# Inducing-point attention and a PReLU layer: token loads and second-attention scores moved to other groups of a hand-ordered schedule

## The chip, the cores and the metric

One core of one Trainium2 chip runs the whole kernel in one launch. The metric is the device time of that core in microseconds (us); the median of five runs of the kernel before is 597.24 us.

The core has TensorE (PE, with weight loads on a row of its own, PEld), VectorE (DVE), ScalarE (ACT), GpSimd (POOL) and SyncE (SP). DMAs are issued in program order from the queues of SP and POOL.

## The reference

Four batches of 12480 tokens with 128 channels attend to and from 32 inducing points; the result runs through a layer of 2048 hidden channels with a PReLU.

```python
B, N, m, C = (4, 12480, 32, 128)
def mab(q, kv):
    s = scale * (q @ kv.transpose(0, 2, 1))
    s = s - s.max(-1, keepdims=True)
    a = np.exp(s)
    a /= a.sum(-1, keepdims=True) + 1e-09
    return a @ kv
h = mab(I, x)              # first attention: 32 inducing points over all tokens of a batch
y = mab(x, h)              # second attention: every token over the 32 rows of h
hid = y @ w_in             # 128 -> 2048
g = np.maximum(hid, 0.0) + alpha * np.minimum(hid, 0.0)
out = g @ w_out            # 2048 -> 128
```

The first attention of a batch must be finished before the second one of that batch starts, so the kernel works on batch n's second attention and layer while it prepares h for batch n+1.

## The kernel before, in words

**Tiles.** A batch is cut into six supers of 2048 tokens (unit numbers 0 to 5) and a remainder of 192 tokens (unit 6). A super has four groups of 512 tokens, and the remainder is a group of its own: 25 groups in a batch, numbered 0 to 24. In the text, "1:17" is group 17 of the second batch (batches count from 0).

**Fills.** The main loop runs over (batch, group, j). One pass of it is a *slot*: j goes over 0 to 3 in a full group and over 0 and 1 in the last, so a batch has 98 slots. In a slot `fill` (L446) makes four matmuls `ring<-rep,hW` (the rows of the second attention's exponentials, `rep`, times h·w_in, `hW`), each into a bank of its own out of a ring of six; ACT (L470) or DVE (L472) empties each bank through a ReLU into `gt`. Then the slot's tasks run, and `mm2` (L476) multiplies the slot before by w_out (`W1`), accumulating 512 tokens of the output in `acc`. The linear part of the PReLU is one 128x128 matrix `Amat`, made at the start by `w_amat` (L684) from `AW` = alpha·w_out and `winT` = the transposed w_in; `linear` (L517) adds it once a group.

**Out.** After a group's last slot, `turn` (L559) lets DVE transpose `acc` into `yT`. When all four groups of a super are there, 16 shuffle DMAs `yq<-yT` (L572) and four `leave` steps (L579 multiplies by the reciprocal denominators, L589 stores) are put on a list, and each slot takes two of its entries. All 20 are POOL's, in order.

**Tasks.** `at(slot, fn, j, cost, narrow)` puts a step into slot (group, j), j being 1 unless it is given. Steps of the next batch's first attention, one of each for each unit u, in the order 0, 1, 6, 2, 3, 4, 5:
- `a_load` (L126): the load of x from HBM with a cast, issued by POOL, not before the ACT instruction that precedes it in the program (`after`);
- `a_xpose` (L155): a transposing DMA `xT<-xn` on SP (L158; L163 for unit 6);
- `a_scores` (L271): four matmuls `ring<-xT,IT`, an exponential on ACT (L277), and a transposing DMA `e1T<-e` on SP (L281);
- `a_accum` (L295): sixteen small matmuls `ring<-xn,e1T` and an addition on DVE (L308).

Steps of the current batch's second attention for each super s: `b_scores` (L363; matmuls `ring<-xT,hT`, an exponential, a store of it to DRAM on SP, L379), `b_rep` (L382; four DMAs back into `rep`, L387), `b_den` (L402; denominators). The order on each engine is pinned to program order (`pin`); semaphores for data and for the reuse of buffers are put in by the framework. A planner (`make_plan`) shares out the evictions between ACT and DVE from the steps' costs.

**Narrow slots.** Where a step with matmuls 32 columns wide runs, `mm2` is issued as 16 matmuls of 32 columns (forms 128*32) in place of four of 128 (128*128).

**Buffers** that matter here: `xn` six, `xT` two (one a batch), `e1T` two, `rep` three, `e2` two, `yT` three, `yq` two, `ob` four.

Of the kernel before, what the change touches and what calls it, by code (L numbers as in the profile page):

```python
# [15 lines left out]
P = 128  # L16
NB = 4
GRP = P * NB
NQ = 4
# [5 lines left out]
def kernel(  # L25
# [11 lines left out]
    bf16 = mybir.dt.bfloat16  # L37

    B, N, C = x.shape
# [9 lines left out]
    KC = DFF // P  # L49
# [20 lines left out]

    const = ctx.enter_context(tc.tile_pool(name="const", bufs=1))
    work = ctx.enter_context(tc.tile_pool(name="work", bufs=2))
    xn_pool = ctx.enter_context(tc.tile_pool(name="xnp", bufs=6))
    xt_pool = ctx.enter_context(tc.tile_pool(name="xtp", bufs=2))
    gt_pool = ctx.enter_context(tc.tile_pool(name="gtp", bufs=4))
    head_pool = ctx.enter_context(tc.tile_pool(name="headp", bufs=3))
# [78 lines left out]
    def a_xpose(st, u):  # L155
        xn = st.xn[u]
        if u < NS:
            pin(nc.sync.dma_start_transpose(  # L158
                out=st.xT[:, u, :, :].rearrange("c q (j p) -> c (q j) p", j=NB),
                in_=xn[:].rearrange("p q f -> p (q f)"),  # L160
            ))
        else:
            pin(nc.sync.dma_start_transpose(  # L163
                out=st.xTr[:], in_=xn[:].rearrange("p j c -> p (j c)")
            ))
# [216 lines left out]
    def b_rep(st, s, q0=0):  # L382
        nq, w = (NQ, GRP) if s < NS else (1, REM)
        rep = rep_pool.tile([P, nq, w], bf16, name="rep", tag="rep" if s < NS else "repr")
        dv = st.d.pop(s)[:].rearrange("(q i) t -> i q t", q=nq)
        for r in range(4):
            pin(nc.sync.dma_start(out=rep[32 * r : 32 * r + 32, q0:], in_=dv[:, q0:]))  # L387
        for q in range(q0, nq):
            st.rep[s * NQ + q] = rep[:, q, :]
# [12 lines left out]
    def b_den(st, s):  # L402
        e2 = st.e2.pop(s)
        ps = bank()
        if s < NS:
            for j in range(NB):
                mm(ps[:, j * NQ : (j + 1) * NQ], e2[:, j * P : (j + 1) * P], pick[:])
            rd = rd_pool.tile([P, NB, NQ], f32, name="rd", tag="rd")
            pin(nc.vector.reciprocal(
                out=rd[:].rearrange("p j q -> p (j q)"), in_=ps[:, : NB * NQ]  # L410
            ))
        else:
            for j in range(JR):
                mm(ps[:PR, j : j + 1], e2[:, j * PR : (j + 1) * PR], pick[0:M, 0:1])
            rd = work.tile([PR, JR, 1], f32, name="rdr", tag="rdr")
            pin(nc.vector.reciprocal(
                out=rd[:].rearrange("p j q -> p (j q)"), in_=ps[:PR, :JR]
            ))
        st.rden[s] = rd
# [233 lines left out]
    alT = const.tile([P, KC], f32, name="alT")  # L653
    om_al = const.tile([P, KC], f32, name="om_al")
    W1 = const.tile([P, KC, C], bf16, name="W1")
    AW = const.tile([P, KC, C], bf16, name="AW")
    winT = const.tile([P, KC, C], bf16, name="winT")
    Amat = const.tile([C, C], bf16, name="Amat")


# [71 lines left out]
    def at(slot, fn, j=1, cost=None, narrow=False):  # L732
        tasks.setdefault((slot, j), []).append((fn, cost))
        if narrow:
            narrows.add((slot, j))
# [12 lines left out]
    for b in range(B):  # L748
        base = b * NG
        for s in range(1, NS + 1):  # L750
            g = base + s * NQ - 4
            at(g, lambda b=b, s=s: b_scores(states[b], s), 3, (215, "A", 490), narrow=True)
            at(g + 1, lambda b=b, s=s: b_rep(states[b], s), 3)
            at(g + 2, lambda b=b, s=s: b_den(states[b], s), 2, (130, "D", 250))
        if b + 1 < B:
            n = b + 1

            def begin(n=n):
                states[n] = new_batch(n)

            for i, u in enumerate(order):
                if b == 0:
                    k, gap = (2, 4, 5, 7, 9, 11, 13)[i], 4
                else:
                    k, gap = base + (-7, -4, -2, 1, 5, 8, 12)[i], 5
                if i == 0:
                    at(k, begin)
                at(k, lambda n=n, u=u: a_load(states[n], u))
                at(k + gap - 2, lambda n=n, u=u: a_xpose(states[n], u))
                at(k + gap, lambda n=n, u=u: a_scores(states[n], u), 0, (215, "A", 680), narrow=True)  # L770
                at(k + gap + 3, lambda n=n, u=u: a_accum(states[n], u), 3, (200, "D", 220), narrow=True)
            k = base + NG - 5
            at(k, lambda n=n: h_sum(states[n]))
            at(k, lambda n=n: h_den(states[n]), 2, (250, "D", 500))
            at(k + 1, lambda n=n: h_transpose(states[n]), 1, (300, "D", 250))
            at(k + 1, lambda n=n: h_weights(states[n]), 3, (215, "D", 600), narrow=True)
            at(k + 2, lambda n=n: b_scores(states[n], 0), 1, (215, "A", 490), narrow=True)
            at(k + 2, lambda n=n: h_linear(states[n]), 3, (80, "D", 250))
            at(k + 3, lambda n=n: b_rep(states[n], 0), 0)
            at(k + 3, lambda n=n: b_den(states[n], 0), 1, (130, "D", 250))  # L780
# [120 lines left out]
```

## Time and profile before

| | |
|---|---|
| median of 5 runs | 597.24 us (594.67 to 602.48) |
| the profiled execution | 602.02 us, of which its span (first to last instruction) 600.0 us |
| mean granted TensorE clock | 0.982 |
| PE busy (as modelled) | 573.1 us, 96% |
| ACT, DVE busy | 510.5 us (85%), 506.4 us (84%) |
| POOL busy | 366.1 us (61%) |
| 18 transposes `xT<-xn`, us from issue to landing (min / median / max) | 4.2 / 6.8 / 10.1 |
| shuffles `yq<-yT` | 368 issues, 0.50 us of POOL each, 3.8 us to landing |

How to read it. The "busy" of PE is modelled, so a slot's length is better read from the timeline: from the start of the four matmuls `ring<-rep,hW` of one fill to the start of the next four. An engine's idle time stands in square brackets in the timeline with what ended it, and in the list of waits in sum. A line such as L99 is a helper's (`mm`), so matmuls are told apart by the tiles that they read and write. The first 25 us are the first attention of batch 0, which no task overlaps; the first fill starts at 24.86 us, and the first fills of batches 1, 2 and 3 at 180.42, 319.06 and 462.11 us.

### The profile page before, as it was taken

To read this page: it belongs to the slowest core of one execution; us is meant where nothing else is said; L and a number is where in the kernel's file an instruction comes from. 1 tells how busy PE (TensorE), PEld (TensorE's weight loads), DVE (VectorE), ACT (ScalarE), POOL (GpSimd) and SP (SyncE) were. 2 spreads that over 40 slices of the span, in tenths; PEclk is the share of its full clock that TensorE was granted. 3 is DMA by queue.
4 is the path that set the end of the run, shared out by engine and by line. 5 is a ranking of instruction groups with operands and counts; after the bars stand their busy time and mean duration, and the time that the engine had idled before them with its cause. 6 is when DMAs were issued, how large, how long until landed. Compare 5 with 4: busy or idle time off the path is not lost.

```text
span 600.0 us, 14389 instructions
## 1 busy us (share of the span) xinstructions
PE 573.1 (96%) x5262; PEld 216.8 (36%) x5262; DVE 506.4 (84%) x849; ACT 510.5 (85%) x1007; POOL 366.1 (61%) x629
## 2 busy tenths in 40 slices
PE   5899996979999999999999899999999999999997
PEld 4533331323343333333334233333334333333366
DVE  3579984868888899989998698989898899999996
ACT  2579994959899898999898799899989999999886
POOL 6612563637757547466864674565885785766754
PEclk9899997989999999999999899999999999999999
DMA  9745788988689696777697879879644543552543
GB/s 196 179 91 111 176 178 179 154 195 176 145 177 191 154 172 154 148 180 176 164 180 144 185 188 133 172 180 164 167 128 120 157 153 105 143 154 89 139 118 135
DMA packets 93638, 93.76 MB, mean 156 GB/s; under 512 B 61328, under 2 KB 76960, under 8 KB 93568
## 3 DMA queue, kind: packets, MB, share of 16 engines
q0 software_dynamic: 24224, 62.39, 43.8%
q1 hardware_dynamic: 69200, 29.94, 25.2%
q8 instruction: 41, 0.67, 0.5%
q10 hardware_dynamic: 144, 0.52, 0.3%
q14 instruction: 29, 0.24, 0.2%
HBM read 40.20 MB, written 28.75 MB: 115 GB/s over the span
## 4 chain that ended last, share of the span: by engine, by line
PE 60%; DMA 18%; POOL 11%; issue 7%; DVE 1%; ACT 1%; SPq 0%; POOLq 0%; ACTq 0%
PE acc L99 41%; PE ring L99 18%; DMA xn<-in_x_dram 10%; DMA yq<-yT 5%; POOL ob L579 4%; POOL yq L572 3%; DMA xT<-xn 3%; POOL out_dram L589 2%; PE ring L187 1%; DMA ind_f<-in_inducing_dram 1%; ACT gt L470 1%; POOL AW L673 1%; POOL W L673 1%; DVE gt L472 1%; DVE xT L193 0%
## 5 line engine op out<-in xcount | busy, mean ns | idle before, releaser
L470 ACT ACTIVATE gt<-ring 128x512 bf16<-128x512 f32 (+1 forms) x919 | 478.8, 600 | 58.9 <-ACT gt L470 27.4
L472 DVE TENSOR_SCALAR gt<-ring 128x512 bf16<-128x512 f32 (+1 forms) x649 | 420.0, 683 | 69.9 <-PE ring L99 61.7
L99 PE MATMUL acc<-gt,W 128*128 128x512 bf16 (+1 forms) x2216 | 387.9, 388 | 0.0
L572 POOL DMA_DIRECT2D yq<-yT x368 | 180.7, 499 | 80.3 <-DMA xn<-in_x_dram 53.2
L99 PEld LDWEIGHTS <-W 128*128 128x128 bf16 (+1 forms) x2216 | 124.1, 98 | 155.1 <-issue 67.9
L99 PE MATMUL ring<-rep,hW 32*128 32x512 bf16 (+1 forms) x1600 | 166.0, 382 | 0.6 <-DVE hW L263 0.2
L579 POOL TENSOR_TENSOR ob<-yq,rd 128x512 f32<-128x512 f32 x92 | 97.0, 1054 | 83.8 <-DMA yq<-yT 82.3
L99 PEld LDWEIGHTS <-hW 32*128 32x128 bf16 x1600 | 44.5, 91 | 164.6 <-issue 159.1
L589 POOL DMA_DIRECT2D out_dram<-ob x92 | 53.7, 584 | 30.3 <-POOL ob L579 27.1
L563 DVE STREAM_TRANSPOSE yT<-acc 128x512 f32<-128x512 f32 x92 | 65.2, 708 | 5.0 <-PE acc L99 4.9
L133 POOL DMA_DIRECT2D xn<-in_x_dram x28 | 15.8, 569 | 27.9 <-ACT gt L470 23.9
L99 PE MATMUL acc<-W,gt 128*128 128x128 bf16 (+1 forms) x384 | 25.6, 220 | 0.0
L99 PEld LDWEIGHTS <-gt 128*128 128x128 bf16 (+1 forms) x384 | 21.9, 106 | 4.1 <-issue 3.6
L277 ACT ACTIVATE e<-ring 128x512 bf16<-128x512 f32 x18 | 10.9, 604 | 8.2 <-PE ring L99 8.2
L99 PE MATMUL acc<-rep,hA 32*128 32x512 bf16 x92 | 17.7, 375 | 0.0
L99 PE MATMUL ring<-xT,IT 128*32 128x512 bf16 x72 | 7.6, 414 | 9.8 <-DMA xT<-xn 9.7
L212 ACT ACTIVATE e1t<-ring 128x256 bf16<-128x256 f32 (+1 forms) x13 | 4.8, 371 | 10.6 <-PE ring L99 10.4
L193 DVE COPY xT<-ring 128x1024 bf16<-128x1024 bf16 (+1 forms) x12 | 8.0, 669 | 5.1 <-PE ring L187 4.6
L369 ACT ACTIVATE e<-ring 128x512 bf16<-128x512 f32 x18 | 10.9, 605 | 0.0
L99 PE MATMUL ring<-xT,hT 128*32 128x512 bf16 (+1 forms) x98 | 10.8, 400 | 0.0
L187 PE MATMUL ring<-ident,xn 128*128 128x128 bf16 x96 | 8.8, 249 | 0.9 <-DVE xn L695 0.9
L99 PEld LDWEIGHTS <-hT 128*32 128x32 bf16 (+1 forms) x122 | 3.7, 93 | 13.0 <-issue 12.9
(92 smaller groups left out, 139.2 us busy)
## 6 DMA issues: line engine op xcount, KB each, us to landing
yq<-yT POOLq DMA_DIRECT2D x368, 64.0 KB, 3.8
out_dram<-ob POOLq DMA_DIRECT2D x92, 256.0 KB, 2.8
rep<-e2d SPq DMA_DIRECT2D x92, 128.0 KB, 3.7
xn<-in_x_dram POOLq DMA_DIRECT2D x18, 512.0 KB, 7.3
e2d<-e SPq DMA_DIRECT2D x24, 128.0 KB, 2.2
xn<-in_x_dram POOLq DMA_DIRECT2D x10, 256.0 KB, 8.6
w_out_f<-in_moe_w_out_dram POOLq DMA_DIRECT2D x4, 256.0 KB, 11.2
out_dram<-obe SPq DMA_DIRECT2D x4, 256.0 KB, 2.3
```

Of the source, the lines that this page charges most:

```text
L99: return pin(nc.tensor.matmul(o, lhsT, rhs, start=start, stop=stop, **kw))
L133: bi = pin(nc.gpsimd.dma_start(out=xn[:, i * w : (i + 1) * w, :], in_=src[:, i * w : (i + 1) * w, :]))
L187: pin(nc.tensor.transpose(tp[:, k * P : (k + 1) * P], xn[:, q, j * C : (j + 1) * C], ident[:]))
L277: pin(nc.scalar.activation(out=e1[:], in_=ps[:], func=EXP, scale=scale, accum_out=st.es[:, u : u + 1]))
L369: pin(nc.scalar.activation(out=e2[:], in_=ps[:], func=EXP, scale=scale_of(st)))
L470: pin(nc.scalar.activation(out=gt[:, r, :w], in_=ps[:, :w], func=RELU))
L472: pin(nc.vector.tensor_relu(gt[:, r, :w], ps[:, :w]))
L563: pin(nc.vector.transpose(out=yT[:, :, q, :, :].rearrange("p a j c -> p j a c"), in_=acc[:].rearrange("p j (a c) -> p j a c", a=4),))
L572: pin(nc.gpsimd.dma_start(out=yq[32 * a : 32 * a + 32, k], in_=yT[32 * k : 32 * k + 32, a]))
L579: pin(nc.gpsimd.tensor_tensor(out=ob[:].rearrange("p j (k c) -> p j k c", k=4), in0=yq[:, :, q].rearrange("p k j c -> p j k c"), in1=bass. ...
L589: pin(nc.gpsimd.dma_start(out=out[t0 : t0 + SUP, :].rearrange("(p q j) c -> q p j c", q=NQ, j=NB)[q], in_=ob[:],))
L673: pin(nc.gpsimd.tensor_tensor(out=dst[:, j::NJ, :], in0=w_out_f[:, j::NJ, :], in1=fb, op=MULT))
```

## The change

Four edits.

1. `xn` has seven buffers in place of six.
2. `AW` and `winT` are no longer tiles of their own; they are the halves of a tile `early` that takes one of the two `yq` buffers at the start.
3. `b_scores` and `b_rep` of supers 2 to 6 run two groups earlier (six groups before the super's first group in place of four); those of super 1, and all `b_den`, stay.
4. The first attention's steps get other slots. Load, transpose, scores and accumulation of units 0, 1, 6, 2, 3, 4, 5 stood at these groups (relative to the current batch):

| | load | transpose | scores | accumulation |
|---|---|---|---|---|
| batch 0 before | 2 4 5 7 9 11 13 | 4 6 7 9 11 13 15 | 6 8 9 11 13 15 17 | 9 11 12 14 16 18 20 |
| batch 0 after | 2 3 4 6 8 10 12 | 5 7 8 10 12 14 15 | 7 9 10 12 14 16 17 | 10 12 13 15 17 19 20 |
| batches 1, 2 before | -7 -4 -2 1 5 8 12 | -4 -1 1 4 8 11 15 | -2 1 3 6 10 13 17 | 1 4 6 9 13 16 20 |
| batches 1, 2 after | -8 -5 -3 0 3 6 9 | -4 -1 1 4 7 10 13 | 0 3 5 8 11 14 17 | 3 6 8 11 14 17 20 |

```diff
-    xn_pool = ctx.enter_context(tc.tile_pool(name="xnp", bufs=6))
+    xn_pool = ctx.enter_context(tc.tile_pool(name="xnp", bufs=7))
...
-    AW = const.tile([P, KC, C], bf16, name="AW")
-    winT = const.tile([P, KC, C], bf16, name="winT")
+    early = yq_pool.tile([P, 2, KC, C], bf16, name="early", tag="yq")
+    AW, winT = early[:, 0], early[:, 1]
...
         for s in range(1, NS + 1):
-            g = base + s * NQ - 4
+            g = base + s * NQ - (6 if s > 1 else 4)
             at(g, lambda b=b, s=s: b_scores(states[b], s), 3, (215, "A", 490), narrow=True)
             at(g + 1, lambda b=b, s=s: b_rep(states[b], s), 3)
+            g = base + s * NQ - 4
             at(g + 2, lambda b=b, s=s: b_den(states[b], s), 2, (130, "D", 250))
...
                 if b == 0:
-                    k, gap = (2, 4, 5, 7, 9, 11, 13)[i], 4
+                    k, t = (2, 3, 4, 6, 8, 10, 12)[i], (7, 9, 10, 12, 14, 16, 17)[i]
                 else:
-                    k, gap = base + (-7, -4, -2, 1, 5, 8, 12)[i], 5
+                    k, t = base + (-8, -5, -3, 0, 3, 6, 9)[i], base + (0, 3, 5, 8, 11, 14, 17)[i]
                 if i == 0:
                     at(k, begin)
                 at(k, lambda n=n, u=u: a_load(states[n], u))
-                at(k + gap - 2, lambda n=n, u=u: a_xpose(states[n], u))
-                at(k + gap, lambda n=n, u=u: a_scores(states[n], u), 0, (215, "A", 680), narrow=True)
-                at(k + gap + 3, lambda n=n, u=u: a_accum(states[n], u), 3, (200, "D", 220), narrow=True)
+                at(min(k + 4, t - 2), lambda n=n, u=u: a_xpose(states[n], u))
+                at(t, lambda n=n, u=u: a_scores(states[n], u), 0, (215, "A", 680), narrow=True)
+                at(t + 3, lambda n=n, u=u: a_accum(states[n], u), 3, (200, "D", 220), narrow=True)
```

## The prediction

> **What bounds the kernel now.** I read the page first (engine shares, clock by slices), then the list of waits, then the timeline around each long wait, on PE, SP and POOL.
>
> ```profile
> PE 573.1 (96%) x5262; PEld 216.8 (36%) x5262; DVE 506.4 (84%) x849; ACT 510.5 (85%) x1007; POOL 366.1 (61%) x629
> ...
> PEclk9899997989999999999999899999999999999999
> ```
>
> PE fills the span, and its granted clock is full but for a few slices. In the timeline a slot without tasks takes 1.30 us, again and again: PE sets the pace, while ACT and DVE have about 15% left. So only what makes PE wait, or gives it more to do, counts. The waits:
>
> ```profile
> DVE gt L472 <- PE ring L99: 61.7, 111, 7.0
> POOL yq L572 <- DMA xn<-in_x_dram: 53.2, 13, 5.9
> ...
> PE ring L99 <- DMA xT<-xn: 9.7, 3, 5.5
> ...
> PE ring L99 <- DMA xTr<-xnr: 2.4, 1, 2.4
> ```
>
> Inside the loop PE waits long for one thing only, the transposed x that the next batch's scores read: four times, 12.1 us. The longest of them:
>
> ```profile
> 78.58 0.56 POOL L133 DMA_DIRECT2D xn<-in_x_dram  x1
> ...
> 79.11 3.45 POOL L572 DMA_DIRECT2D yq<-yT  x7
> ...
> 85.92 2.47 SPq L158 DMA_TRANSPOSE xT<-xn  x1
> ...
> 86.18 0.50 POOL L572 DMA_DIRECT2D yq<-yT  x1 [3.62 <-DMA xn<-in_x_dram]
> 86.97 0.57 POOL L133 DMA_DIRECT2D xn<-in_x_dram  x1 [0.28 <-issue]
> ...
> 90.17 0.40 PE L99 MATMUL ring<-rep,hW 32*128 32x512 bf16 x4
> ...
> 96.02 0.62 PE L99 MATMUL ring<-xT,IT 128*32 128x512 bf16 x4 [5.45 <-DMA xT<-xn]
> ...
> 96.42 1.92 PE L99 MATMUL acc<-gt,W 128*32 128x512 bf16 x16
> ...
> 98.28 0.61 PE L99 MATMUL ring<-rep,hW 32*128 32x512 bf16 x4
> ...
> 100.64 0.42 PE L99 MATMUL ring<-rep,hW 32*128 32x512 bf16 x4
> ```
>
> Unit 2's load stands in slot 0:7 (from 67.6 us) but leaves POOL at 78.58, behind the `leave` steps of super 0, and lands at 85.9. Only then can SP issue the transpose, which takes 10.1 us with the next load issued beside it. PE, ready at 90.5, stands until 96.02. POOL's lines show why loads are late: after a load seven shuffles go out, and the eighth waits until the load has landed. POOL has no pause for want of work from 55 to 487 us.
>
> **What each stall costs.** I compare slots, since after the gap the clock is down too (16 narrow matmuls take 1.92 us). An undisturbed scores slot:
>
> ```profile
> 325.47 0.40 PE L99 MATMUL ring<-rep,hW 32*128 32x512 bf16 x4
> ...
> 325.79 0.40 PE L99 MATMUL ring<-xT,IT 128*32 128x512 bf16 x4
> ...
> 326.02 1.04 PE L99 MATMUL acc<-gt,W 128*32 128x512 bf16 x16
> ...
> 326.99 0.48 PE L99 MATMUL ring<-rep,hW 32*128 32x512 bf16 x4
> ```
>
> It takes 1.52, and with the plain slot behind it 2.82. Stall 1 (0:11): 90.17 to 100.64 is 10.47, so 7.65 lost. Stall 2 (0:15): 120.63 to 128.73, 8.10, so 5.28. Stall 3 (2:3, unit 6): 336.94 to 343.61, 6.67; the same two slots of batch 1 take 2.90, so 3.77. Stall 4 (2:17): 2.19 against 1.52, 0.67. Together 17.4. A check: first fill to first fill, batch 1 takes 138.64 and batch 2 143.05, 4.41 more; stalls 3 and 4 make 4.44.
>
> **The change part by part.**
>
> *Seventh xn buffer:* the new first attention holds a load for at most 11 groups in place of 8, three or four alive, so six would have done: 0.
>
> *AW and winT in a yq buffer:* the buffer is free after `w_amat` in slot 1 (about 38 us); its next user is super 1, whose shuffles begin at 79.1. That hides the wait; without it, POOL would stand. Were the two halves treated as one write, the `winT` transposes (issued 30.11) would wait for POOL's `AW` (ends 32.09): up to +2. I take 0, as 16 shuffles into one yq tile go out without waiting for each other. Below 0 nothing, as nothing is taken away.
>
> *Scores of supers 2 to 6 two groups earlier:* the same four matmuls (a slot of 1.52 in place of 1.30), one ACT pass of 0.6, one store and four `rep` DMAs on SP, passing only the other SP steps of those two groups. PE's waits for `rep` sum to 0.6 in the whole loop, so nothing is to be won; `rep`'s third buffer is free in time (its last reader is at least three groups back). 0, between -0.6 and +0.6.
>
> *First attention, batches 1 and 2.* Load to scores becomes 8 groups (8 x 5.7 = 45.6 us) in place of 5, transpose to scores 4 in place of 2. The worst delays of this trace: unit 6's load stands in 1:23 (312.2) and leaves POOL at 331.31, 19 late; loads land in at most 10.6, transposes in 10.1. 40 is less than 45.6, so stalls 3 and 4 go: -4.4. Next late after these is `rep` (0.6 in all).
>
> *First attention, batch 0.* Loads get 5 or 6 groups in place of 4. Unit 2's load now stands in slot 6, after the 16 shuffles (the last ends at 66.6) but before the `leave` steps: it leaves near 67 in place of 78.6. Unit 4's likewise goes ahead of super 1's `leave` steps, unit 3's goes before super 1's shuffles (78), unit 5's before super 2's (100). All land at least 10 us before their scores (at 96, 107, 118, 124). But the transposes keep their two groups, and on SP each waits behind the previous unit's `e1T`: a scores slot at 325.47 has its `e1T` issued at 327.63, and that takes 1.2, so the transpose goes 3.4 into the slot. Two groups are 11.3, the matmuls come 0.3 into theirs: 8.2 are left. Landing takes 4.2 to 10.1, median 6.8. Best: no stall. Worst: 10.1 four times (units 1 to 4), 1.9 each and 1.4 to 1.8 for the slow clock (what stalls 3 and 2 lost beyond their idle 2.4 and 3.7), so some 15. I take 1.5, nearer the median's end (one miss of middling size): the 10.1 belonged to a transpose with a load issued 1.05 later, and the new loads leave POOL some 4 us away from a transpose or more. Stalls 1 and 2: -12.9, +1.5.
>
> The Trainium skill has a rule against this part (DMA: Bandwidth & Descriptors, Issuing engines are not separate DMA queues): DMAs from all engines run on the same 16 DMA engines and interleave, so a load brought forward is paid by the transposes it meets. By that rule in full, at 10.1 for all four, the sum would be about 600 in place of 587. Another page (TensorE: Matmul & The Clock Gate, The HAM clock gate) lets the clock drop after an idle window of about 3.4 us; this trace shows it at half pace after 2.4 (16 narrow matmuls 2.04 in place of 1.04), so the measured price is used.
>
> *Narrow slots.* An accumulation alone lengthens its slot by 0.33 (329.67 to 331.30 against 1.30), in a slot shared with `b_scores` by 0.22 (1.95 against 1.73). Shared ones go from 3 to 1 in batch 0 and from 3 to 2 in batches 1 and 2: four lost, 0.11 to 0.17 each: +0.5.
>
> *SP's new wait.* In batch 0, unit 5's `e1T` (slot 17, j 0) needs the buffer that unit 3's accumulation frees in slot 17, j 3: SP stands some 4 us. Behind it is super 6's store, a group later; unit 5's accumulation comes three groups later (17 us), and `e1T` lands in at most 10.2. 0.
>
> *POOL's queue:* the same DMAs. Big loads followed by eight or more shuffles, where POOL waits, are 12 of 18 by the new order, about 14 before: 0 or a little less.
>
> Sum against the profiled execution: 602.0 - 4.4 - 12.9 + 1.5 + 0.5 = 586.7, so **587**. That execution lies 4.8 above the median of five (597.24). Stalls that hang on landing times may differ from run to run, and the new kernel has them no more, so I let 587 stand; if the stalls were equal in all runs, 597.2 - 15.3 = 581.9, near the low end.
>
> **The rivals.**
>
> *A. The transposes of batch 0 stay late* (two to four misses at 3.5, so 7 to 14 in place of 1.5): 592 to 600. For it: 8.2 of room against landings up to 10.1. Against: of the 18 transposes only three took over 8.4, and two of these had a load issued beside them.
>
> *B. The loads come no earlier,* because POOL, always busy, reaches them no sooner: 597 to 602. Against: the new places are ahead of `leave` steps or of whole shuffle runs.
>
> *C. Slower: POOL becomes the bound.* POOL took 432 us for 18 supers (55.2 to 487.2), 18.9 each where no load runs (508.9 to 527.8), so 92 for 18 loads, 5.1 each. With PE 17.4 sooner, POOL's lag at super 3:0 would grow from 0.3 to 17.7; DVE's `yT` (three buffers) stands still at a lag near 34 (nine groups, 51, less 17 for shuffles and landing). That is reached at 6.0 a load; at 7.0, the dearest seen, the lag is 52, the stall 18, the time 604. For it: no pause on POOL. Against: fewer loads are followed by shuffles.
>
> **How the numbers follow.** Likeliest, stalls gone with at most a small rest (581 to 590): 0.66. A 0.16, B 0.07, C and anything else slower 0.09; below 581, 0.02. A measurement tells about 1% from no change (591.3 to 603.2): faster 0.66 + 0.02 + 0.05 of A = 0.73, same 0.11 + 0.07 = 0.18, slower 0.09. The range 581 to 597 leaves out B, C, the end of A and what lies below: 2 in 10; the likeliest case's own is 581 to 590.
>
> **What would show it.** Right: PE's waits for `xT` and `xTr` under 2 us in all, batches 1 and 2 equal within 1 us, no clock dips after 60 us, batch 0 about 13 shorter. Wrong: waits for `xT` at 0:9, 0:12, 0:14 or 0:16 (A); loads leaving POOL as late as before (B); DVE's `yT` or PE's `acc` waiting for shuffles near the end of batch 2 (C).

## The result, and the profile after

Predicted were 587 us, with a range of 581 to 597. Measured: a median of 598.33 us over 44 runs (587.27 to 619.63), against 598.81 for the kernel before over 79 runs (592.96 to 604.32). The ratio of after to before is 0.992, 95% interval 0.9894 to 0.9946, but it is taken over the executions within 1.5% of each kernel's fastest, 9 of the 44 after and 72 of the 79 before, so it flatters a kernel whose times scatter. The medians of all runs differ by 0.1%: no gain that can be told, and 587 was 11 us too low. What did change is the scatter: 32 us from best to worst, against 11 before.

The profiled execution took 597.30 us, its span 595.3 (before 602.02 and 600.0), at the same mean clock of 0.982. The two lines of the page that answer to those shown of before:

```profile
PE 573.4 (96%) x5298; PEld 218.5 (37%) x5298; DVE 501.5 (84%) x841; ACT 514.1 (86%) x1015; POOL 365.9 (61%) x629
...
PEclk9899999799999999999997999999999999999999
```

PE is as full as before, and two slices of the clock are still down inside the loop (the two 7s): the eighth, 104 to 119 us, and the 22nd, 313 to 327 us. Those are the two places to look at. The list of waits of after (who waited, for what; us in total, times, longest):

```profile
POOL yq L572 <- DMA xn<-in_x_dram: 41.1, 12, 5.4
...
POOL yq L572 <- DVE yT L563: 23.4, 6, 4.5
...
PE ring L99 <- DMA xT<-xn: 5.0, 1, 5.0
...
PE ring L99 <- DMA rep<-e2d: 2.7, 4, 1.5
```

The wait for `xTr` is gone, that for `xT` is one in place of three, and one for `rep` has come. POOL waits longer for DVE's `yT` than in before, which means that it has caught up more often and stands for want of work, not that it is behind. The same line of before:

```profile
POOL yq L572 <- DVE yT L563: 12.6, 5, 3.2
```

The lengths of the batches, from first fill to first fill, say where the time went; the last column is batch 3 from its first fill to the end of the span:

| | batch 0 | batch 1 | batch 2 | batch 3 |
|---|---|---|---|---|
| before | 155.6 | 138.6 | 143.1 | 137.8 |
| after | 150.3 | 138.7 | 144.1 | 137.7 |

The four places where PE stood before are all clear (0:11, 0:15, 2:3 and 2:17 have their plain lengths). Two new ones have come. The first, in the timeline of after:

```profile
101.17 3.85 SPq L158 DMA_TRANSPOSE xT<-xn  x1
...
103.45 0.56 POOL L133 DMA_DIRECT2D xn<-in_x_dram  x1
...
106.41 0.44 PE L99 MATMUL ring<-rep,hW 32*128 32x512 bf16 x4
...
111.80 0.62 PE L99 MATMUL ring<-xT,IT 128*32 128x512 bf16 x4 [4.95 <-DMA xT<-xn]
112.20 1.92 PE L99 MATMUL acc<-gt,W 128*32 128x512 bf16 x16
...
114.06 0.61 PE L99 MATMUL ring<-rep,hW 32*128 32x512 bf16 x4
...
116.42 0.61 PE L99 MATMUL ring<-rep,hW 32*128 32x512 bf16 x4
```

This is unit 3's score step in 0:14. Its data is in SBUF early (the load left POOL at 76.18), but the transpose still goes out two groups ahead, at 101.17; unit 5's load is issued 2.3 us behind it, the transpose needs 10.6 us, and PE stands 4.95 us and then runs at half pace. 106.41 to 116.42 is 10.01 for two slots that take 2.82 undisturbed: 7.19 lost. The second new place is the first slot of batch 2:

```profile
301.24 0.56 POOL L133 DMA_DIRECT2D xn<-in_x_dram  x1
...
302.36 0.34 SPq L379 DMA_DIRECT2D e2d<-e  x1
...
310.90 1.75 SPq L387 DMA_DIRECT2D rep<-e2d  x4
...
313.45 0.37 PE L99 MATMUL ring<-rep,hW 32*128 32x512 bf16 x1 [0.31 <-DMA rep<-e2d]
...
320.14 0.61 PE L99 MATMUL ring<-rep,hW 32*128 32x512 bf16 x4
...
322.21 0.39 PE L99 MATMUL ring<-rep,hW 32*128 32x512 bf16 x4
```

Here the load is unit 1's, now eight groups ahead of its scores, and the store `e2d<-e` of the new batch's super 0 goes out 1.1 us after it. The store lands at 310.85, 8.5 us later; the four `rep` DMAs follow at once and land up to 317.14, and PE takes them one by one as they come. In before a load went out close to this store too, but 0.35 us behind it, and the store landed after 2.2 us:

```profile
308.10 0.34 SPq L379 DMA_DIRECT2D e2d<-e  x1
308.45 0.57 POOL L133 DMA_DIRECT2D xn<-in_x_dram  x1 [0.40 <-ACT e L369]
```

In after, 313.45 to 322.21 is 8.76; the same two slots take 2.99 in batch 1: 5.77 lost, and 0.38 more in 1:24.

So 17.4 went and 7.19 + 5.77 + 0.38 = 13.3 came back: 602.0 - 17.4 + 13.3 = 597.9, against 597.3 measured.

### The profile page after: what moved, and what is told of

It reads as the page before. It is cut to its first block, busy times and chain, and to the rows that moved or that the text cites. A ratio compares the mean times of both kernels' runs of the same rounds, so it can differ in the third digit from the quotient of the medians.

```text
span 595.3 us, 14460 instructions
## 1 busy us (share of the span) xinstructions
PE 573.4 (96%) x5298; PEld 218.5 (37%) x5298; DVE 501.5 (84%) x841; ACT 514.1 (86%) x1015; POOL 365.9 (61%) x629
## 4 chain that ended last, share of the span: by engine, by line
PE 90%; DMA 6%; ACT 2%; DVE 1%; issue 1%; SPq 0%; POOL 0%; ACTq 0%; POOLq 0%
PE acc L99 62%; PE ring L99 27%; DMA xn<-in_x_dram 3%; DMA xT<-xn 2%; ACT gt L470 2%; DMA rep<-e2d 1%; DVE gt L472 1%; ACT e L369 0%; POOL xn L133 0%; SPq L387 0%; DVE hW L263 0%; DVE yT L563 0%; PE ring L187 0%; ACT xT L195 0%; DVE obe L548 0%
## 5 line engine op out<-in xcount | busy, mean ns | idle before, releaser
L472 DVE TENSOR_SCALAR gt<-ring 128x512 bf16<-128x512 f32 x641 | 415.5, 683 | 70.3 <-PE ring L99 61.8
L99 PE MATMUL acc<-gt,W 128*128 128x512 bf16 (+1 forms) x2252 | 386.1, 384 | 0.0
L99 PEld LDWEIGHTS <-W 128*128 128x128 bf16 (+1 forms) x2252 | 124.1, 98 | 153.0 <-issue 66.3
L99 PE MATMUL ring<-rep,hW 32*128 32x512 bf16 (+1 forms) x1600 | 166.5, 382 | 3.1 <-DMA rep<-e2d 2.7
L99 PEld LDWEIGHTS <-hW 32*128 32x128 bf16 x1600 | 44.4, 91 | 167.4 <-issue 158.7
L133 POOL DMA_DIRECT2D xn<-in_x_dram x28 | 15.7, 567 | 23.4 <-ACT gt L470 19.3
L99 PE MATMUL acc<-W,gt 128*128 128x128 bf16 (+1 forms) x384 | 26.5, 224 | 0.0
L99 PEld LDWEIGHTS <-gt 128*128 128x128 bf16 (+1 forms) x384 | 22.6, 109 | 4.3 <-issue 3.8
L99 PE MATMUL acc<-rep,hA 32*128 32x512 bf16 x92 | 17.6, 375 | 0.0
L277 ACT ACTIVATE e<-ring 128x512 bf16<-128x512 f32 x18 | 10.8, 602 | 7.8 <-PE ring L99 7.8
L99 PE MATMUL ring<-xT,IT 128*32 128x512 bf16 x72 | 7.6, 414 | 5.0 <-DMA xT<-xn 5.0
L99 PE MATMUL ring<-xT,hT 128*32 128x512 bf16 (+1 forms) x98 | 10.7, 394 | 0.4
L99 PEld LDWEIGHTS <-hT 128*32 128x32 bf16 (+1 forms) x122 | 4.4, 93 | 12.0 <-issue 11.7
```

The costliest lines, as they stand in the source:

```text
L99: return pin(nc.tensor.matmul(o, lhsT, rhs, start=start, stop=stop, **kw))
L133: bi = pin(nc.gpsimd.dma_start(out=xn[:, i * w : (i + 1) * w, :], in_=src[:, i * w : (i + 1) * w, :]))
L277: pin(nc.scalar.activation(out=e1[:], in_=ps[:], func=EXP, scale=scale, accum_out=st.es[:, u : u + 1]))
L472: pin(nc.vector.tensor_relu(gt[:, r, :w], ps[:, :w]))
```

## The experiments

The question was where the expected gain went. *Theory 1:* transfers that stand only two groups ahead of their use, batch 0's transposes and a batch's first `rep`, land late when another transfer meets them; the loads were moved off the stalls of before and into others. *Rival 2:* the clock, or something else that more lead won't cure. *Rival 3:* the earlier `b_scores` and `b_rep` (edit 3) hold up the transposes on SP's queue. In later runs theory 1 was split: *1a*, the load beside the transfer is what makes it late; *1b*, shuffles and stores do, or the place behind `rep` on SP; *1c*, only the lead counts. Diffs are against the kernel after; where a kernel is built on another experiment, that is said. Ratios are against the kernel before, run beside it on the same chip, with 95% intervals, and are taken in the same way as above.

| kernel | median us (range, runs) | ratio | batches 0, 1, 2 in its trace |
|---|---|---|---|
| again | 595.39 (585.05 to 608.32, 6) | none taken | 157.6, 146.1, 140.6 |
| no_edit3 | 597.47 (592.35 to 601.67, 12) | 0.9949 (0.9912 to 0.9986) | 156.0, 138.5, 138.9 |
| xpose4 | 585.77 (584.06 to 589.74, 6) | 0.9772 (0.9721 to 0.9823) | 141.3, 139.5, 139.7 |
| xpose4_b | 588.28 (585.89 to 594.82, 6) | 0.9823 (0.9776 to 0.9871) | 140.9, 138.4, 141.9 |
| h_early | 600.42 (592.27 to 610.88, 12) | 0.9958 (0.9912 to 1.0004) | 150.0, 139.2, 139.2 |
| front_loads | 591.62 (585.32 to 603.15, 6) | 0.9825 (0.9772 to 0.9879) | 150.2, 138.4, 138.4 |
| xpose3 | 588.94 (581.84 to 594.62, 6) | 0.976 (0.9706 to 0.9814) | 142.6, 138.5, 142.9 |
| xpose4_h | 587.65 (584.32 to 592.9, 6) | 0.9792 (0.9746 to 0.9838) | 144.3, 139.1, 139.4 |
| old_batch0 | 598.26 (595.8 to 604.79, 12) | 0.9965 (0.9935 to 0.9996) | 156.7, 138.6, 138.4 |
| load_waits | 596.63 (592.2 to 601.28, 12) | 0.9946 (0.991 to 0.9981) | 151.2, 141.7, 138.4 |
| x4_waits | 594.32 (588.36 to 596.78, 9) | 0.9903 (0.9868 to 0.9938) | 147.1, 140.4, 143.2 |
| x4_front | 591.38 (588.15 to 593.87, 6) | 0.9866 (0.9826 to 0.9905) | 142.9, 141.5, 142.9 |
| load18 | 596.11 (589.69 to 602.84, 12) | 0.9913 (0.9875 to 0.9951) | 153.6, 138.4, 138.4 |
| x4_load18 | 582.97 (581.86 to 583.91, 6) | 0.9731 (0.9692 to 0.9769) | 141.1, 138.4, 138.4 |
| x4_load18_h | 586.26 (584.53 to 586.71, 6) | 0.9781 (0.9739 to 0.9823) | 143.9, 139.0, 139.4 |

Batch 3 is 137.5 to 138.1 in all of them. Two numbers such as 3.27 + 2.23 are the lengths in us of a group's first slot and of the one behind it; undisturbed, the two take 2.8 to 3.0. Differences of up to about 2 us in batch 0 prove nothing: its first ten slots took 15.4 to 17.8 us, by whether the granted clock was at half for 0, 3.4 or 6.8 us from 23 to 27 us on.

### again: the same kernel once more

No edit.

> The changed kernel once more, unchanged, for a second trace and as the yardstick for the others. Theory 1 (DMAs with only two groups of lead land late in some executions: the x transposes of batch 0, and the rep of a batch's first super): 592 to 600 us, with 1 to 3 PE waits of 2 us or more inside the loop, on xT in batch 0 or on rep at a batch's first slot, not always at the same unit as in the first trace. Theory 2 (something other than waits, such as the clock, lengthens the executions): the waits sum to under 2 us and the time is still 595 or more. Theory 3 (the rep DMAs, two groups earlier, stand on SP and hold the transposes behind them): the PE wait is again at unit 3 (0:14), behind a rep that waits for its store.

Two executions of one program differ by 11 us (spans 595.3 and 606.3), and by which transfer was late. The timeline of this trace, at the place of the first stall:

```profile
101.11 3.74 SPq L158 DMA_TRANSPOSE xT<-xn  x1
101.36 0.56 POOL L133 DMA_DIRECT2D xn<-in_x_dram  x1
...
118.81 0.62 PE L99 MATMUL ring<-xT,IT 128*32 128x512 bf16 x4 [11.40 <-DMA xT<-xn]
```

The load now leaves 0.25 us behind the transpose, in place of 2.3, and the transpose takes 17.7 us in place of 10.6; the load lands after 15.5 (POOL's next shuffle, which waits for it, goes at 117.11). In batch 1 it happens again: transpose at 222.29, load at 222.52; they take 25.0 and 24.5. The `e1T` issued at 230.87 then takes 25.3, and PE waits for the transpose in 1:11, four groups behind it, and for `e1T` in the accumulation. A wait for `xTr`, gone in the first trace, is back too (2.0 us at 0:10). The start of batch 2, where the profiled run of after lost 5.77, lost 2.19 here (5.18 for the two slots), and not by the store, which took 2.6: a load went out 0.3 us ahead of the four `rep` DMAs, which took 7.4 to 9.1. What is late hangs on a meeting of DMAs that fractions of a microsecond decide.

### no_edit3: supers 2 to 6 back at four groups

```diff
-            g = base + s * NQ - (6 if s > 1 else 4)
+            g = base + s * NQ - 4
```

> The changed kernel with the second attention's scores and rep back in their old slots (edit 3 undone). Theory 3: the wait at unit 3 in batch 0 goes, and the time falls by about 7 us against the changed kernel. Theory 1: no difference beyond 3 us; waits for xT in batch 0 or for rep at a batch's start are still there in the trace. Theory 2: no difference.

The waits for `xT` stay: 10.5 us in three times, the longest 8.4 at 0:12, another at 0:16. Rival 3 falls. The longest:

```profile
86.36 7.04 SPq L158 DMA_TRANSPOSE xT<-xn  x1
88.40 0.50 POOL L572 DMA_DIRECT2D yq<-yT  x1 [5.75 <-DMA xn<-in_x_dram]
...
103.12 0.62 PE L99 MATMUL ring<-xT,IT 128*32 128x512 bf16 x4 [8.37 <-DMA xT<-xn]
```

This transpose took 16.7 us, and a load was in flight for its first 1.8 us alone. What ran beside it afterwards were shuffles: the eight that left from 88.40 to 92.72 took 10.2 to 11.0 us each, against a median of 3.8 in before.

Batch 1 is 138.5 and batch 2 138.9, so edit 3 by itself is worth nothing that these runs can tell.

### xpose4 and xpose4_b: batch 0's transposes four groups ahead of their scores

```diff
-                at(min(k + 4, t - 2), lambda n=n, u=u: a_xpose(states[n], u))
+                at((t - (3 if u == 5 else 4) if b == 0 else k + 4), lambda n=n, u=u: a_xpose(states[n], u))
```

> The changed kernel with batch 0's x transposes four groups ahead of their scores in place of two (unit 5 three groups); loads and everything else as in the changed kernel. Theory 1: PE's waits for xT in batch 0 are gone, 4 to 7 us less than the changed kernel on average; a wait for rep at a batch's first slot can stay. Theory 2: no difference. Theory 3: half of it, since the transposes of units 2 to 4 now stand ahead of the rep on SP.

Batch 0 shrinks to 141.3: 0:14 and the slot behind it take 2.9 in place of 10.0 (-7.1), and the rest of the 9.0 lies in the first slots, where the granted clock stayed full. The clock line of the page is full:

```profile
PEclk9999999999999999999999999999999999999999
```

The transposes did not become quicker. Those issued from 75 to 135 us, in the trace's own words on that line of the program:

```profile
DMA to landing us min/median/max: 6.7/9.1/12.1
```

These are three; with two groups, 8.2 us of room, two of them would have been late, and with four none is. This speaks for lead and against rival 2.

> The early transposes alone once more (585.8 us before), as the yardstick on the same chip as the other three: 584 to 589 us.

The same kernel a second time: batch 0 is 140.9, again without a wait, but batch 2 is 141.9, with 3.27 + 2.23 in 2:4 and the slot behind it, for `rep`. The part of theory 1 about transposes holds in both; the rest of the gain wobbles with `rep`.

### xpose3: three groups

```diff
+                at((t - 3 if b == 0 else k + 4), lambda n=n, u=u: a_xpose(states[n], u))
```

> The changed kernel with batch 0's transposes three groups ahead of their scores, between two (changed kernel) and four (585.8 us). Theory 1 with room worked out from the traces (8.2 us at two groups, some 14 at three, 19 at four; landings so far 4 to 17.7): most waits gone, 586 to 590 us. If only the exact place of a load beside a transpose counts and not the room: anything between 585 and 598.

Three groups are enough in this trace (landings of batch 0: 6.2 to 9.6, no wait for `xT`). What is left is 2:0, 4.57 + 2.29: the store at 294.83 landed after 8.2, with a load issued 1.3 us before it, as in after.

### front_loads: batch 0's loads in the first groups, transposes where they were

```diff
-                    k, t = (2, 3, 4, 6, 8, 10, 12)[i], (7, 9, 10, 12, 14, 16, 17)[i]
+                    k, t = (2, 2, 2, 3, 3, 4, 4)[i], (7, 9, 10, 12, 14, 16, 17)[i]
...
+                at(((5, 7, 8, 10, 12, 14, 15)[i] if b == 0 else k + 4), lambda n=n, u=u: a_xpose(states[n], u))
```

> The changed kernel with batch 0's loads all at groups 2 to 4 (two groups' worth of POOL's idle time and of quiet DMA queues) in place of 2 to 12; transposes and scores stay where the changed kernel has them, two groups apart. Theory 1a (the transposes of batch 0 land late because a load leaves POOL beside them): they land in 4 to 9 us after 75 us of the span, PE's waits for xT in batch 0 go, 584 to 589 us. Theory 1b (they land late because of shuffles and stores, or sit too long behind rep on SP): landings of 10 us or more and waits stay, 592 to 599 us.

From 75 us on no load is in flight in batch 0, and the transposes, still two groups ahead, take 4.4, 5.1 and 8.8 us (least, median, most); no wait for them. But the very first transpose meets two loads (and the ends of two more):

```profile
52.99 12.47 SPq L158 DMA_TRANSPOSE xT<-xn  x1
53.22 1.05 POOL L133 DMA_DIRECT2D xn<-in_x_dram  x2 [4.11 <-ACT gt L470]
...
72.64 0.62 PE L99 MATMUL ring<-xT,IT 128*32 128x512 bf16 x4 [6.20 <-DMA xT<-xn]
```

It takes 19.6 us, the loads 15.1 and 16.8, and PE loses its slots there (8.84 + 2.22). That fits 1a on both sides, but it doesn't test it against shuffles, which the expectation names under 1b: four of the five transposes after 75 us had no shuffle issued in their first 4 us either, and the first one had six.

### h_early: h of the next batch one group earlier

```diff
-                    k, t = (2, 3, 4, 6, 8, 10, 12)[i], (7, 9, 10, 12, 14, 16, 17)[i]
+                    k, t = (2, 3, 4, 6, 8, 10, 12)[i], (7, 9, 10, 12, 14, 15, 16)[i]
...
-                    k, t = base + (-8, -5, -3, 0, 3, 6, 9)[i], base + (0, 3, 5, 8, 11, 14, 17)[i]
+                    k, t = base + (-8, -5, -3, 0, 3, 6, 9)[i], base + (0, 3, 5, 8, 11, 14, 16)[i]
...
-            k = base + NG - 5
+            k = base + NG - 6
```

> The changed kernel with the end of the first attention one group earlier (unit 5's scores in group 16 in place of 17, in batch 0 unit 4's in 15; the sums, h and the first super's scores and rep in groups 19 to 22 in place of 20 to 23). Theory 1: no PE wait for rep at a batch's first slot, 2 to 4 us less than the changed kernel on average, while waits for xT in batch 0 stay. Theory 2 and 3: no difference.

The store of super 0's scores and its `rep` go one group earlier, and the wait at the batch's start is gone (batches 1 and 2 are 139.2 each). Batch 0 keeps a stall, now at 0:15 (6.75 + 2.37), where unit 4's scores went. That lead cures the wait for `rep` is seen directly at 2:0: the store went out 1.2 us behind a load and took 8.4 us, and the first two slots still took 3.1. That it pays in time is not shown (ratio up to 1.0004, median 600.42 against 599.99 for the kernel before beside it).

**xpose4_h** is xpose4 with this edit.

> The two earlier ones together: batch 0's transposes four groups ahead, and the end of the first attention with the first super's scores and rep one group earlier. Theory 1: no PE wait for xT, xTr or rep over 1 us in the loop, 582 to 586 us, 1 to 3 us less than the early transposes alone (there the waits for rep cost about 2.8 us). If rep's waits are luck: the same as the early transposes alone.

No wait for `rep`, 0.8 for `xT`, batch 0 144.3: no better than xpose4, whose batch 0 is 3.0 us shorter.

### old_batch0: batch 0's slots as before, the rest as after

```diff
-                    k, t = (2, 3, 4, 6, 8, 10, 12)[i], (7, 9, 10, 12, 14, 16, 17)[i]
+                    k, t = (2, 4, 5, 7, 9, 11, 13)[i], (6, 8, 9, 11, 13, 15, 17)[i]
```

> The changed kernel with the slots of batch 0 as before the change (loads 2 4 5 7 9 11 13, scores 6 8 9 11 13 15 17, transposes two groups ahead); batches 1 and 2 and the second attention as changed. Theory 1: waits for xT in batch 0 as large as in the kernel before or the changed one (7 to 15 us), 593 to 599 us; batches 1 and 2 without waits for xT or xTr. If the changed slots of batch 0 were a loss by themselves: under 590 us.

Batch 0 is back at 156.7 with its old stalls (0:11 with 10.2 + 2.37, 0:15 with 4.54 + 2.37); batches 1 and 2 are 138.6 and 138.4. The edits of batches 1 and 2 do what was predicted of them when nothing meets the store.

### load_waits and x4_waits: the loads wait for the transposes

```diff
+                    if xposed:
+                        tc.add_manual_dep(
+                            bi.ins, xposed[-1],
+                            mybir.DependencyInfo(
+                                mybir.DependencyClass.Sync, mybir.DependencyReason.DATA
+                            ),
+                            reason="not beside a transpose",
+                        )
```

A load of batches 1 to 3 waits until the last transpose issued ahead of it in the program (`xposed` collects them) has landed. The lines of this kernel lie ten below those of after (L168 is the transpose).

> The changed kernel, in which each load of batches 1 to 3 also waits until the last x transpose before it in program order has landed, so that no load leaves POOL beside a transpose that it follows; slots, and the two groups between transposes and scores in batch 0, as in the changed kernel. So far transposes with a load issued within 0.5 us after them took 14.6 to 25.0 us to land (4 cases), within 0.5 to 3 us 9.5 in the middle, with none 6.4. Theory 1a (the load beside it makes the transpose late, and the two groups would do without that): transposes of batch 0 land in 4 to 9 us, PE's waits for xT in batch 0 sum to under 2 us, 584 to 589 us. Theory 1c (only the lead counts; the load beside it is a bystander): waits for xT stay, 593 to 599 us. Rival: POOL, standing at the loads, falls so far behind that loads come late and PE waits for them in batches 1 and 2: over 599 us.

The waits for `xT` stay, 7.8 us in three times, so 1a's expectation failed. For the longest of them the timeline says why it tells nothing against 1a either:

```profile
94.91 0.57 POOL L133 DMA_DIRECT2D xn<-in_x_dram  x1 [5.39 <-ACT gt L480]
98.09 6.02 SPq L168 DMA_TRANSPOSE xT<-xn  x1
...
111.17 0.62 PE L99 MATMUL ring<-xT,IT 128*32 128x512 bf16 x4 [4.98 <-DMA xT<-xn]
```

A load that was held back until a transpose had landed (at 94.33; the bracket names an ACT instruction, which came last) is in flight when the next transpose goes out, 3.2 us behind it, and that one takes 13.0. Here holding back one partner only moved the meeting. The wait at 0:16 (1.2 us) had a load 2.2 us ahead of its transpose; the one at 0:17 (1.6 us) had no load in flight at all: its transpose, of 11.6 us, ran beside shuffles and the end of the transpose before it. So a load is not needed for a late transpose, and the run doesn't separate 1a from 1c.

**x4_waits** is xpose4 with the same wait.

> The same waiting loads with batch 0's transposes four groups ahead. If lead and distance each do the work alone: the same as the early transposes alone, 584 to 588 us, no more to win in batch 0. If landings over 14 us still cost something in batches 1 and 2: 1 to 2 us less, and a smaller spread.

It is slower than xpose4 (0.9903 against 0.9772, intervals apart): there are waits at 0:17 (5.36 + 2.3, for `xT`), 1:0 (3.72) and 2:0 (5.66 + 2.14), the last two for `rep`, with a load 1.4 us ahead of the store each time. The expected 584 to 588 was missed.

### x4_front: loads in front and transposes early

```diff
-                    k, t = (2, 3, 4, 6, 8, 10, 12)[i], (7, 9, 10, 12, 14, 16, 17)[i]
+                    k, t = (2, 2, 3, 3, 4, 6, 8)[i], (7, 9, 10, 12, 14, 16, 17)[i]
...
+                at((t - (3 if u == 0 else 4) if b == 0 else k + 4), lambda n=n, u=u: a_xpose(states[n], u))
```

> The changed kernel with batch 0's loads at groups 2 2 3 3 4 6 8 in place of 2 3 4 6 8 10 12, and its transposes four groups ahead (unit 0 three). Loads then use the time in which POOL has nothing to do (33 to 54 us). Theory 1: 583 to 587 us, no wait for xT in batch 0; not told apart from the early transposes alone unless POOL's lag mattered there.

Batch 0 (142.9) gains nothing over xpose4's 141.3: with four groups of lead it makes no difference that can be told where the loads lie (a wait of 1.0 us is left at 0:7, whose transpose has three groups). Batches 1 and 2 spend 4.73 in 1:0's first slot and 5.27 + 2.14 in 2:0, waiting for `rep`; in both a load was again issued just ahead of the store (1.1 and 1.3 us). The expected 583 to 587 was missed by these.

### load18: the load beside the store moved away, the store left where it is

```diff
-                    k, t = base + (-8, -5, -3, 0, 3, 6, 9)[i], base + (0, 3, 5, 8, 11, 14, 17)[i]
+                    k, t = base + (-9, -7, -3, 0, 3, 6, 9)[i], base + (0, 3, 5, 8, 11, 14, 17)[i]
...
-                at(min(k + 4, t - 2), lambda n=n, u=u: a_xpose(states[n], u))
+                at((min(k + 4, t - 2) if b == 0 else base + (-4, -1, 1, 4, 7, 10, 13)[i]), lambda n=n, u=u: a_xpose(states[n], u))
```

> The changed kernel with the loads of units 0 and 1 for batches 2 and 3 at groups -9 and -7 (16 and 18 of the batch before) in place of -8 and -5; transposes, scores and batch 0 as changed. In the changed kernel unit 1's load leaves POOL within 2 us of the store of the next batch's first exponentials, the rep that waits for it comes late, and PE loses up to 6 us at a batch's first slot. Theory (that meeting is the cause): no such wait, batches 1 and 2 both 138 to 140 us; batch 0 still 150 to 157; in all 591 to 599, some 2 us under the changed kernel and too little to tell in the time alone. Rival (the rep there is late whatever is loaded): first slots of 3 us and more again.

Batches 1 and 2 take 138.4 each and PE waits for no `rep`, though store and `rep` keep their lead. By itself this trace proves little, since no_edit3, front_loads and old_batch0, with unit 1's load at -5, have no wait there either. All 17 traces together say more. Of their 34 starts of batches 1 and 2, ten had a load of a full unit issued 0.5 to 2.7 us ahead of the store: the store then took 6.2 to 8.5 us. In the eight of these with the usual lead the first two slots took 4.1 to 8.8 us; in the two with a group more (h_early, xpose4_h) 3.1 and 3.0. In the other 24 the store took 1.7 to 5.4 us, and only one start was late by more than 0.8, again's. So it is the load just ahead of the store that makes `rep` late, and load18's move takes it away. Batch 0, untouched, keeps its stalls (0:14 with 11.92 + 2.07). Its list of waits:

```profile
PE ring L99 <- DMA xT<-xn: 10.0, 2, 9.2
...
PE ring L99 <- DMA xTr<-xnr: 1.2, 1, 1.2
```

### x4_load18: both cures

Both edits, xpose4's in batch 0 and load18's in batches 1 and 2:

```diff
+                    k, t = base + (-9, -7, -3, 0, 3, 6, 9)[i], base + (0, 3, 5, 8, 11, 14, 17)[i]
...
+                at((t - (3 if u == 5 else 4) if b == 0 else base + (-4, -1, 1, 4, 7, 10, 13)[i]), lambda n=n, u=u: a_xpose(states[n], u))
```

> The same loads with batch 0's transposes four groups ahead. Theory: batches of about 141, 138.5 and 138.5 us, 582 to 586 us, 1 to 3 us under the early transposes alone (585.8 and 588.3 in two runs). Rival: the same as those.

582.97 us, the fastest of all and the steadiest (2 us from best to worst), 2.7% below the kernel before (2.3 to 3.1%) and faster than the kernel after. Its page, and the one line in its list of waits where PE's `ring` matmuls of L99 wait for a DMA:

```profile
PE 565.2 (97%) x5298; PEld 216.8 (37%) x5298; DVE 500.4 (86%) x841; ACT 513.6 (88%) x1015; POOL 367.0 (63%) x629
...
PEclk9999999999999999999999999999999999999999
```

```profile
PE ring L99 <- DMA early<-w_in_b: 0.4, 1, 0.4
```

PE is *less* busy than in after (565.2 against 573.4) with the same 5298 matmuls, since none in the loop runs at half pace, neither at its start nor behind a gap. The transposes still take 5.3 to 13.5 us (median 8.5).

**x4_load18_h** adds h_early's edit, against the last rival, that a batch's first `rep` is late whatever is loaded beside its store.

> Besides, the end of the first attention and the next batch's first scores and rep one group earlier. Theory: nothing more to win than with the loads moved, 582 to 586 us. Rival (rep late whatever is loaded): this one is faster than the one without it by 1 to 3 us.

Nothing is won (143.9, 139.0, 139.4): there was no wait for `rep` left, so that rival falls. Batch 0 is 2.8 us longer, 0.9 of it in the first ten slots; most of the rest lies in one slot of the squeezed scores, 0:16 with j 2, which takes 2.95 us and in which PE waits 0.78 for the exponential of the scores (ACT, L277).

### What the runs settle

Lead cures the waits for the transposes (none left in xpose3, xpose4, xpose4_b and x4_load18; 0.8 and 1.0 us in xpose4_h and x4_front; only where loads are held back, in x4_waits, 3.8), and loads kept away from the store, or a group more of lead, cure the wait for `rep`. With both, x4_load18 takes 582.97 us, no longer than the 587 that was expected of the change.

What stretches a transpose is less settled. The 306 transposes `xT<-xn` of all 17 traces, sorted by the loads of full units in flight with them:

| load | transposes | median us | least to most |
|---|---|---|---|
| none in flight | 186 | 6.5 | 4.2 to 14.9 |
| issued over 3 us behind | 66 | 8.0 | 5.8 to 16.7 |
| only ahead, still in flight | 21 | 10.0 | 5.8 to 15.1 |
| issued 0.5 to 3 us behind | 29 | 9.5 | 5.3 to 12.1 |
| issued within 0.5 us behind | 4 | 18.6 | 14.6 to 25.0 |

A load goes with a late transpose, then, but it isn't the only thing that does: of the 186 without a load 41 took more than the 8.2 us that two groups leave. Shuffles go with those. With at most three shuffles issued in the transpose's first 5 us it was 14 of 134 (median 6.2), with four or more 27 of 52 (median 8.3, the longest 14.9). All this is a sorting of traces; a kernel that forces one meeting and leaves the others out wasn't built. Which partner makes a transpose late in a given place, and why both partners stretch, stays open.

## Why the prediction was wrong

**The bound, and what gave way: right.** "So only what makes PE wait, or gives it more to do, counts" held in every run, and the 17.4 us of the four stalls are gone from their four places. The sum less its rest, 602.0 - 4.4 - 12.9 + 0.5 = 585.2, is what a kernel without late transposes should take: xpose4 took 585.77 and 588.28, and x4_load18 582.97. (The 602.0 lies 3.2 above the median of the 79 runs; from 598.8 the same terms give 582.0.)

**The term that failed: "I take 1.5, nearer the median's end".** In its place stand 7.19 us in the profiled run of after, 11 to 14 in other traces with two groups (again's 0:14: 14.1 + 2.37 against 2.82; load18's: 11.92 + 2.07). The step behind it was: "Landing takes 4.2 to 10.1, median 6.8", so the worst was to be 1.9 of idle time a unit. (The 1.8 there for the slow clock should read 1.6: stall 2 lost 5.28, of which 3.68 was idle. The worst case changes by less than 1 us.) The 10.1 was the largest of 18 transposes of one execution, not a bound: the next traces have 16.7, 17.7, 19.6 and 25.0. And the ground for the low end, "the new loads leave POOL some 4 us away from a transpose or more", is the sharper error. A load's slot doesn't say when it leaves: in the two traces of after unit 5's load left POOL 2.3 and 0.25 us behind unit 3's transpose. POOL's queue places it, behind shuffles that wait for loads and stores. (In the traces of before, after and again POOL's DMAs take eight completion semaphores in turn, numbers 99 to 106; that is why the eighth DMA behind a load waits for the load.) Where loads are brought forward into a queue that is always busy, each move shifts later ones too. I had the meeting in hand (the 10.1 "belonged to a transpose with a load issued 1.05 later") and used it as a reason for optimism.

**The second term that failed: "PE's waits for `rep` sum to 0.6 in the whole loop, so nothing is to be won", and "Next late after these is `rep` (0.6 in all)".** It was costed as a thing that edit 3 might mend, not as one that edit 4 might break. Unit 1's load, moved to -5, left at 301.24, and the store of the next batch's super 0, which edit 3 doesn't move, went out 1.1 us later and took 8.5 us. Cost: 5.77 + 0.38. The prediction named what SP's moved steps pass on SP's queue; it didn't ask what each moved *load* would newly lie beside. That eats the gain of stalls 3 and 4 in batch 2 whole (143.1 before, 144.1 after).

**Rival A** had the right mechanism, and with 7 to 14 about the right price, though in the profiled run it was one large miss and not two to four of 3.5; it lacked the meeting with the store. That its 592 to 600 holds the median is in part luck: 6.15 us of the profiled run are the store's. **Rival B** is refuted: in batch 0 the loads of units 3, 4 and 5 left POOL at 76.18, 89.47 and 103.45, against 86.97, 107.92 and 116.08 before. **Rival C** too: POOL waited more for work, not less.

**The edits costed at nothing** cost nothing: the narrow slots' +0.5 and edits 1 to 3 together are within 0.1 us in batch 1 (138.6 to 138.7) and in batch 3 (137.8 to 137.7), where no stall hides them; the larger part of the +0.5, in batch 0, can't be told from the rest there. `early` made PE wait 0.3 to 0.6 us at the start in some traces. SP's new wait isn't seen among PE's waits.

**The criteria** "waits for `xT` and `xTr` under 2 us in all", "batches 1 and 2 equal within 1 us", "no clock dips after 60 us" and "batch 0 about 13 shorter" were missed (5.0 us; 138.7 and 144.1; two dips; 5.3 shorter). The wait for `xT` at 0:14 points at A, as written; nothing in the list named `rep`.

The rule that the prediction set against the change, from the Trainium skill (DMA: Bandwidth & Descriptors, Issuing engines are not separate DMA queues), was weighed at "about 600 in place of 587" and came nearer than the trace's median did. Loads of POOL and transposes of SP do slow each other down here. But taking turns on the same engines doesn't explain the size: in the worst meeting the engines moved less in all (56 GB/s; the last section has the numbers), not the same amount shared.

## What to carry to other kernels

Give a transfer that the busiest engine waits for the lead of its worst landing, taken over several executions and beside whatever else may be in flight, not the median or the maximum of one trace; here two more groups of lead on batch 0's transposes and the loads of two units moved away from a store were worth 15 us on top of the change (598.33 to 582.97). When loads are moved forward, list for each what it will newly be issued beside, by the time at which its queue lets it go and not by its slot, and price that meeting too. If two runs of one kernel differ by ten microseconds, compare them batch by batch: what moves is what hangs on a meeting.

## What the hardware showed that I had not expected

In the four meetings of a transpose of 512 KB with a casting load issued within half a microsecond behind it, the transposes took 14.6 to 25.0 us and the loads 9.4 to 24.5; loads with no transpose in flight took 5.0 to 9.9, with a median of 6.5 (184 of them, from 30 us on). In again, at the meeting at 222 us, stretches of the span before and in it (columns: stretch, its length, busy us of PE, PEld, DVE, ACT and POOL with instructions, granted clock, DMA share, GB/s):

```profile
215.00:222.00 7.00, 7.00 (x78) 2.54 (x76) 5.94 (x11) 6.58 (x13) 3.89 (x9) 1.00 0.64 117
228.00:234.00 6.00, 6.00 (x60) 2.09 (x52) 4.99 (x10) 5.87 (x14) 4.49 (x6) 1.00 1.32 56
```

The DMA engines' share of busy time doubles, to more than all of the time, while they move 56 GB/s in place of 117. Packets of SP's queue took 122 ns on average from 222 to 247 us, against some 23 ns from 101 to 112 us in after. It is a part of the packets that is slow: half of SP's still took 22 ns or less, and the 481 of 2638 that took over 200 ns make up 72% of that queue's time. And the transpose and the load are not alone in it: four `rep` DMAs, four stores of the output and three shuffles issued from 226 to 238 us took 18 to 23 us each. What the slow packets wait for, and whether the load or something else set it off, no run here shows.

The start of the loop varies by itself: its first ten slots took 17.6 us in the profiled run of after and 15.7 in x4_load18. In after the granted clock is at half from 24.9 to 31.7 us, and an `mm2` of four matmuls takes 1.9 us; in x4_load18 it is full, and the same step takes 1.0. No edit between the two touches those slots.
